# Attention of an adaLN block: row blocks in the outer loop in place of head groups, with the output projection at two-unit spacing and the modulation sums among the projections

## The chip, the cores and the metric

The kernel runs on one core of a Trainium2 chip. The metric is the device time of one execution in microseconds. Engines are called as the profile names them: PE (TensorE, matrix products), DVE (VectorE), ACT (ScalarE), POOL (GpSimd) and SP (SyncE, which issues most of the transfers).

## The reference

The input x has 2048 rows of 576 numbers. Six modulation vectors come from one conditioning row. Attention has 32 heads of 18 numbers and a causal window of 256 rows; then comes a spatial-shift mixer and an MLP (hidden width 4608).

```python
mod = (silu(c) @ w_mod).reshape(1, 6, 1, -1)
sa, ca, ga, sb, cb, gb = (mod[:, n] for n in range(6))
h = layernorm(x) * (1 + ca) + sa
q, k, v = split(h @ wqkv)                # 32 heads of 18
p = softmax(where(0 <= i - j < 256, q @ k.T * 18 ** -0.5, -1e9))
x = x + ga * ((p @ v) @ wo)              # output projection
h = layernorm(x) * (1 + cb) + sb
x = x + gb * B(h)                        # shift mixer, then gelu MLP
```

## The kernel before

The 2048 rows are 16 row tiles of 128 and, for attention, four row blocks g = 0 to 3 of 512. The 32 heads are four groups c = 0 to 3 of eight; each group has two halves hq of four heads. All fp32 products are made of three split (high and low) products.

**Projections.** Normalised rows are multiplied with the V, Q and K weights (`vproj` L406, `qproj` L422). Q and K go to DRAM (`qkh`, `qkl`).

**Attention.** One unit is one (c, g, hq), 32 in all. `uload` (L451) brings its Q and K with 12 transfers on SP's queue into a tile U, of which there are four. `s2` makes 16 score products `sc` (PE, L477) and their row maxima (DVE, L484); then the maxima go into the U tile (`mr` on DVE, L490 and L491). `s3` of the unit makes the products `X` (L526, L527), the exponentials (ACT, L533), `av` (PE, L548) and the copy `avs` (ACT, L553), and transposes and normalises the result into the tile `o`. `s3` of one unit runs beside `s2` of the next. With the second half of a head group, `o` is stored to DRAM as `od`[g] (L570). A block g=0 has only 512 rows of keys, the others 768. Before the change the loops are c outside, g inside, hq innermost, so unit n is 8c + 2g + hq: units 0, 1, 8, 9, 16, 17, 24 and 25 have g=0, and the output rows of every block are complete only in the last head group.

**Output projection.** `s4(g, i)` does row tile t = 4g + i in steps at the offsets `d4`, in units of about 12 us: load `or` from `od` and the input row tile `xr` (SP); transposes `oTT` (PE L68 and L72, with ACT copies and DVE L70, L74); two halves of 14 matmuls with `Wo` (PE L763) and the additions to `xr` (DVE L764); store `xp`; row statistics; modulation in two DVE instructions (L99, then L101, `ln1`); store `hbd`; statistics; normalisation (L886, `ln2`); store `xnd`. The three stores are L769 on SP. `woload` multiplies the rows of `Wo` with `ga` and splits them (POOL). The steps of block 3 are played in the next stage.

**Modulation.** `modvec(v)`, v = 2 to 5, loads five chunks of `w_mod`, multiplies and adds them on POOL, sums over partitions with four matmul records on PE (L215) and stores the vector.

**What sets the order.** Each step is an event with a time in units; `play()` emits them in the order of these times. For PE, POOL and SP the written order is the program order. For DVE and ACT the framework's scheduler chooses it. A transfer on SP whose data isn't ready holds all transfers written behind it.

Of the kernel before, what the change touches and what calls it, by code (L numbers as in the profile page):

```python
# [27 lines left out]
NCH = H // CH  # L28
# [22 lines left out]
class Kern:  # L51
# [54 lines left out]
    def row(self, name):  # L106
        return self.rp.tile([P, D], F32, tag="r", name=name, bufs=self.b_row)
# [19 lines left out]
    def phase_a(self):  # L127
# [9 lines left out]
        NGA = 4  # L137
        self.nb = {"sc": self.b_sc, "st": self.b_st, "tr": 1, "av": 1}
        with ExitStack() as st:
# [11 lines left out]
            units = []  # L151
# [74 lines left out]
            def warm(k):  # L226
                def f():
                    pw = self.ps.tile([P, 512], F32, tag="sc", name=f"pw{k}", bufs=self.b_sc)
                    for _ in range(self.n_warm[k]):
                        nc.tensor.matmul(pw, self.zb, self.zb.unsqueeze(1).to_broadcast([P, 4, P]), start=True, stop=True)  # L230
                return f
# [207 lines left out]
                return f  # L439

            def unit(c, g, hq):
                return units[(2 * g + hq) % 4]

            def uload(c, g, hq):
                def f():
                    q, k = unit(c, g, hq)
                    h0 = 8 * c + 4 * hq

                    def put(dst, row, src, first, r, c0, c1, eng=nc.sync):
                        v = src[first:first + 4 * DH, c0:c1].rearrange("(j r d) n -> d j r n", r=2, d=DH)[:, :, r, :]  # L450
                        eng.dma_start(dst[row:row + DH].bitcast(F32), v)  # L451

                    c0, c1 = max(0, g * 512 - 256), g * 512 + 512
                    kd = k[:, :, 768 - (c1 - c0):]
                    for r in range(2):
                        for n, src in enumerate((qkl, qkh, qkh)):
                            put(kd, 64 * r + n * DH, src, D + h0 * DH, r, c0, c1)
                        for n, src in enumerate((qkh, qkh, qkl)):
                            put(q[:, r::2, :], 64 * r + n * DH, src, h0 * DH, r, g * 512, c1, nc.scalar if c == g == hq == 0 else nc.sync)
                return f  # L460

            KR = P - 2

            def s2(c, g, hq):
                QZ, KZ = unit(c, g, hq)
                box = []
                reds = {}
# [36 lines left out]

            def s3(c, g, hq):
                QZ, KZ = unit(c, g, hq)
                Pb, Xb, abox = {}, {}, []
                banks = [0, 3, 1, 2] if g else [3, 1, 2]
# [114 lines left out]
            s4 = self.s4  # L623

            def sub2(c, g, hq, tb):
                st, f1, f2 = s2(c, g, hq)
                return [(tb + 0.95 * t / 16, f) for t, f in st] + [(tb + 0.96 + 0.06 * self.lt, f1), (tb + 1.05 + self.l_m, f2)]

            def sub3(c, g, hq, tb):
                st, n, f1, f2, f3 = s3(c, g, hq)  # L630
                e = max(t for t, _ in st) / n * self.ww
                return [(tb + self.ww * t / n, f) for t, f in st] + [(tb + e + self.l_f, f1), (tb + e + self.l_f + self.l_o, f2), (tb + e + self.l_f + self.l_o + self.l_s, f3)]
# [3 lines left out]
            T0 = -16.2  # L636
            ev = [(T0 - 1.99, lambda: lns[0][0]()), (T0 - 1.98, consts), (T0 - 1.975, cond), (T0 - 1.97, warm(0))]
# [24 lines left out]
            for kind, a, b in jobs:  # L662
                g = a // 4 if kind == "v" else b
# [14 lines left out]
            for t in range(4, NT):  # L678
                g, i = divmod(t, 4)
                ld, stt, nm, tr = lns[t]  # L680
# [15 lines left out]
                ev.append((ta[n], ualloc(n)))  # L696
            shift = self.t_end + self.u0

            u = 0
            for c in range(NCH):  # L700
                for g in range(NGA):
                    for hq in range(2):
                        tb = 2 * u + hq + shift
                        n = 2 * u + hq
                        tu = tb - self.u_ld
                        ev.append((max(tu, ta[n] + 0.01) if n < 4 else tu, uload(c, g, hq)))
                        ev.append((tb - 0.001, lambda c=c, g=g, hq=hq, tb=tb: sub2(c, g, hq, tb)))
                        ev.append((tb + self.o3 - 0.001, lambda c=c, g=g, hq=hq, tb=tb + self.o3: sub3(c, g, hq, tb)))
                    if c == NCH - 1:
                        for i in range(4 if g < 3 else 0):  # L710
                            t4 = 2 * u + shift + 1.2 + self.o3 + self.ww + self.l_av / 16 + self.l_f + self.l_o + self.l_r + 0.5 * i - self.d4[0]
                            ev += [(t4 + d, f) for d, f in s4(g, i)]
                    u += 1
            uw = 2 * (3 * NGA) - 0.6 + shift
            wb, steps = woload()
            ev.append((uw, wb))
            for k, (ld, ml, sp) in enumerate(steps):
                ev += [(uw + 0.05 + 0.4 * k, ld), (uw + 0.45 + 0.4 * k, ml), (uw + 0.5 + 0.4 * k, sp)]
            for n, v in enumerate((2, 3, 4, 5)):
                steps, spill, store = modvec(v)  # L720
                t0 = shift + 5.0 + 4.2 * n
                for k, (ld, ch) in enumerate(steps):
                    ev += [(t0 + 0.35 * k, ld), (t0 + 0.35 * k + 0.4, ch)]
                ev += [(t0 + 3.7, spill), (t0 + 3.9, store)]
            tw = 2 * u - 0.1 + shift
            wb, steps = self.load_w1()
            ev.append((tw, wb))
            w2 = self.load_w2()
            for n, (ld, f) in enumerate(steps + w2):
                d = 0.17 if n < len(steps) else 0.08  # L730
                t0 = tw + 0.17 * min(n, 10) + 0.08 * max(0, n - 10)
# [4 lines left out]
    def s4(self, g, i):  # L736
        nc, rp, row, Wo = self.nc, self.rp, self.row, self.Wo
        t = 4 * g + i
        box = {}

        def load():
            box["o"] = row(f"or{t}")
            nc.sync.dma_start(box["o"], self.od[g][i * P:(i + 1) * P, :])
            box["x"] = row(f"xr{t}")
            nc.sync.dma_start(box["x"], self.x[t * P:(t + 1) * P, :])

        def tr():
            box["T"] = rp.tile([P, 2 * KC + 1, P], F32R, tag="oT", name=f"oT{t}", bufs=1)
            self.split9(box["o"], box["T"], slice(0, P), f"oTT{t}", ("sc", "st") if g < 3 else ("tr", "tr"))

        def wo(hf):
            def f():
                T, x = box["T"], box["x"]
                cs = slice(hf * 288, (hf + 1) * 288)
                tag = ("sc", "st")[hf] if g < 3 else "mm"
                po = self.ps.tile([P, 288], F32, tag=tag, name=f"po{t}_{hf}", bufs=self.nb[tag])
                pl = []
                for k in range(KC):
                    h, l = Wo["m"][:, k, cs], Wo["m"][:, KC + k, cs]
                    pl += [(T[:, k, :], h), (T[:, k, :], l), (T[:, KC + k, :], h)]  # L760
                pl += [(T[:, 2 * KC, :], Wo["h"][:, cs]), (T[:, 2 * KC, :], Wo["l"][:, cs])]
                for n, (l, r) in enumerate(pl):
                    nc.tensor.matmul(po, l, r, start=(n == 0), stop=(n == len(pl) - 1))  # L763
                nc.vector.tensor_tensor(out=x[:, cs], in0=po, in1=x[:, cs], op=ALU.add)  # L764
            return f

        def put(d):
            def f():
                nc.sync.dma_start(d[t], box["x"])  # L769
            return f  # L770

        def stat(k):
            def f():
                box["s"] = self.stats(box["x"], f"{k}{t}")
            return f

        def ln1():
            x = box["x"]
            self.modulate(x, x, *box["s"], self.cb, self.sb, self.m_s4)

        def ln2():
            x = box["x"]
            self.norm_t(x, x, *box["s"])
        d = self.d4
        return list(zip(d, (load, tr, wo(0), wo(1)))) + [(d[3] + self.l_p, put(self.xp)), (d[4], stat("b")), (d[4] + self.l_n, ln1), (d[4] + self.l_n + self.l_p, put(self.hbd)), (d[5], stat("c")), (d[5] + self.l_n, ln2), (d[5] + self.l_n + self.l_p, put(self.xnd))]
# [395 lines left out]
    u0, u_ld = -1.55, 1.3  # L1181
    e_ld, e_tr, e_w2, e_x1, e_lt, e_s4 = 1.2, 0.7, 1.2, 0.8, 0.8, 0.0
    d4 = (-0.2, 0.1, 0.38, 0.56, 0.85, 1.2)
    l_r = 0.4
    c_w, c_t = 8.1, 8.6
    lt, l_e, l_av, l_f, l_o = 1.2, 0.1, 0.0, 0.1, 0.12
    l_m = 0.1
# [34 lines left out]
```

## Time and profile before

| | |
|---|---|
| median of 3 runs | 1789.46 us (1785.65 to 1795.23) |
| the profiled execution | 1788.75 us, its span 1786.9 us |
| projections, dense on PE | about 20 to 222 us |
| attention units | about 196 to 658 us |
| shift mixer | 688 to 865 us |
| MLP, PE-bound | from 865 us on |

PE is busy for 97% of the span. A stretch in which PE stands or runs at a lower granted clock is thus a stretch of the result. The row `avs` (L553) comes once in each unit and marks the units in time.

### The profile page before, as it was taken

The numbers are of one execution on the slowest core, as the hardware profiler recorded it, in microseconds if no ns is written. First come the engines' busy times: TensorE is split into PE (matmuls) and PEld (weight loads), VectorE is DVE, ScalarE is ACT, GpSimd is POOL, SyncE is SP. The second block draws the span as 40 slices with busy tenths as digits, with TensorE's granted clock in tenths as the row PEclk, the third lists the DMA queues.
The fourth block names the chain that finished last, engine by engine and source line by source line (L and its number), as shares of the span: only waits on it lengthen the run. The fifth ranks groups of instructions, "written<-read, shape, count | busy, mean of one in ns | idle before, by whom it ended". The sixth has DMA issues, their size and how long they took to land.

```text
span 1786.9 us, 30143 instructions
## 1 busy us (share of the span) xinstructions
PE 1731.2 (97%) x11700; PEld 1501.8 (84%) x11700; DVE 977.6 (55%) x2674; ACT 594.5 (33%) x1262; POOL 390.1 (22%) x379
## 2 busy tenths in 40 slices
PE   7999999999998988999899999999999999999999
PEld 5898767677767768899799999999999999999998
DVE  5402387778777875877544444444444444444434
ACT  4622166666664444354211111111111111111111
POOL 5511102222030110201432333234421121122100
PEclk8999999999999997999999999999999999999999
DMA  6434544544444556632211111111110000000002
GB/s 178 122 101 155 181 124 134 136 118 140 119 139 126 172 176 190 202 101 78 86 48 35 42 55 40 36 49 55 55 35 16 29 26 16 29 29 29 1 1 106
DMA packets 97712, 156.88 MB, mean 88 GB/s; under 512 B 11035, under 2 KB 40479, under 8 KB 97571
## 3 DMA queue, kind: packets, MB, share of 16 engines
q1 hardware_dynamic: 86612, 135.12, 25.5%
q10 hardware_dynamic: 10958, 19.85, 3.1%
q8 instruction: 92, 1.51, 0.4%
q14 instruction: 50, 0.40, 0.1%
HBM read 107.06 MB, written 47.20 MB: 86 GB/s over the span
## 4 chain that ended last, share of the span: by engine, by line
PE 55%; DVE 2%; POOL 0%; issue 0%; DMA 0%; ACT 0%; SPq 0%; POOLq 0%; ACTq 0%; DVEq 0%
PE p L1147 26%; PE p L1118 22%; PE p L1120 2%; PE p L1119 2%; PE w L1012 2%; PE pg L959 2%; DVE x L1013 0%; DMA r<-in_B_w_dram 0%; DVE G L977 0%; POOL CW L1102 0%; DVE LNT L70 0%; DVE CW L1097 0%; DVE xm L886 0%; DVE G L964 0%; DVE Gc L1129 0%
## 5 line engine op out<-in xcount | busy, mean ns | idle before, releaser
L1147 PEld LDWEIGHTS p<-CW,Gc 128*128 128x128 f32 x3456 | 473.8, 188 | 16.2 <-DVE Gc L1129 3.7
L1147 PE MATMUL p<-CW,Gc 128*128 128x288 f32 x3456 | 482.0, 295 | 3.5 <-DVE Gc L1129 3.5
L1118 PE MATMUL p<-LNT,CW 128*128 128x512 f32 x1728 | 419.1, 391 | 0.0
L1118 PEld LDWEIGHTS p<-LNT,CW 128*128 128x128 f32 x1728 | 316.2, 188 | 58.8
L1126 ACT ACTIVATE gfc<-p 128x512 f32<-128x512 f32 x144 | 86.2, 599 | 735.5 <-PE p L1120 735.5
L1151 DVE TENSOR_TENSOR acc<-p,acc 128x288 f32<-128x288 f32 x340 | 153.8, 455 | 319.2 <-PE p L1147 315.9
L484 DVE CUSTOM_DVE_ANT_0 sc<-sc,mask 128x384 f32<-128x384 f32 (+2 forms) x512 | 261.8, 555 | 84.1 <-PE sc L477 81.3
L533 ACT ACTIVATE P<-X 128x384 f32<-128x384 f32 x480 | 221.8, 490 | 107.9 <-PE X L527 94.5
L477 PE MATMUL sc<-U 126*128 126x384 f32 (+2 forms) x512 | 197.8, 404 | 5.5 <-DVE m L484 3.9
L526 PE MATMUL X<-U 128*128 128x384 f32 (+2 forms) x704 | 181.9, 317 | 4.8 <-DMA U<-ms 1.9
L1151 DVE TENSOR_TENSOR accw<-p,accw 128x288 f32<-128x288 f32 x204 | 90.0, 453 | 129.5 <-PE p L1147 128.1
L526 PEld LDWEIGHTS X<-U 128*128 128x128 f32 x704 | 126.7, 191 | 35.3 <-issue 23.9
L527 PE MATMUL X<-maskb,identb 128*128 128x256 bf16 x480 | 136.1, 284 | 0.0
L1129 DVE TENSOR_TENSOR Gc<-gfc,Gc 128x512 fp32r<-128x512 f32 x144 | 124.8, 867 | 4.5
L422 PE MATMUL pq<-hT,Wq 128*128 128x512 f32 x504 | 122.0, 400 | 2.3 <-POOL Wq L380 1.6
L422 PEld LDWEIGHTS pq<-hT,Wq 128*128 128x128 f32 x504 | 95.0, 190 | 24.8 <-POOL Wq L380 1.9
L477 PEld LDWEIGHTS sc<-U 126*128 126x128 f32 x512 | 98.5, 197 | 13.4 <-DVE m L484 9.6
L1098 POOL TENSOR_TENSOR CW<-r,CW 128x1024 fp32r<-128x1024 f32 x17 | 41.5, 2440 | 283.2 <-DVE CW L1096 283.2
L548 PE MATMUL av<-P,V 128*32 128x256 f32 (+2 forms) x1472 | 91.0, 379 | 0.0
L1128 ACT CAST Gc<-gfc 128x512 fp32r<-128x512 f32 x144 | 89.4, 621 | 4.6
L1102 POOL TENSOR_TENSOR CW<-r,CW 128x1152 fp32r<-128x1152 f32 x17 | 46.4, 2728 | 158.3 <-DVE CW L1101 158.3
L527 PEld LDWEIGHTS <-identb 128*128 128x128 bf16 x480 | 46.0, 96 | 36.0 <-issue 18.6
(1056 smaller groups left out, 1973.5 us busy)
## 6 DMA issues: line engine op xcount, KB each, us to landing
U<-qkh SPq DMA_DIRECT2D x156, 72.0 KB
U<-qkh SPq DMA_DIRECT2D x96, 108.0 KB
r<-in_B_w_dram SPq DMA_DIRECT2D x18, 576.0 KB
qkh<-hl ACTq DMA_DIRECT2D x36, 256.0 KB
qkl<-hl ACTq DMA_DIRECT2D x36, 256.0 KB
r<-in_B_w_dram SPq DMA_DIRECT2D x18, 512.0 KB
U<-qkl SPq DMA_DIRECT2D x78, 72.0 KB
U<-qkl SPq DMA_DIRECT2D x48, 108.0 KB
```

What stands on the lines that cost most here:

```text
L422: nc.tensor.matmul(pq, a, b, start=(n == 0), stop=(n == len(pl) - 1))
L477: nc.tensor.matmul(sc[:, lo:], QZ[:KR, q, i * P:(i + 1) * P], KZ[:KR, j, i * P + lo:(i + 3) * P], start=True, stop=True)
L484: nc.vector.tensor_tensor_reduce(out=sc[:, lo:], in0=sc[:, lo:], in1=mask[:, lo:], scale=1.0, scalar=-3e38, op0=ALU.add, op1=ALU.max, accu ...
L526: nc.tensor.matmul(X[:, x0:x0 + nb, :].rearrange("p a b -> p (a b)"), KZ[:, j, kb * P:(kb + 1) * P], QZ[:, q, qb * P:(qb + nb) * P], start ...
L527: nc.tensor.matmul(X[:, 0::2, :], self.identb, mk, start=False, stop=True)
L533: nc.scalar.activation(Pb[b][:, q, :], Xb[b, q].rearrange("p a b -> p (a b)"), AF.Exp, scale=SCALE)
L548: nc.tensor.matmul(abox[0][32 * q:32 * q + 32, q0:q0 + w], V[4 * g + kb][:, hv:hv + 32], Pb[b][:, q, p0:p0 + w], start=(first and n == 0), ...
L1118: nc.tensor.matmul(pg, W3[:, ws, fs], L[:, xs, :], start=(i == 0), stop=False)
L1128: nc.scalar.copy(Gh, gf)
L1129: nc.vector.tensor_tensor(out=Gl, in0=gf, in1=Gh.bitcast(F32), op=ALU.subtract)
L1147: nc.tensor.matmul(po, a, w, start=(i == 0), stop=(i == len(seq) - 1))
L1151: nc.vector.tensor_tensor(out=acc[t][:, cs], in0=po, in1=acc[t][:, cs], op=ALU.add)
```

## The change

The loops of attention go over g outside and c inside, so unit n is 8g + 2c + hq, and the first eight units have g=0. The output of block g is complete after its eight units; the four steps s4(g, 0 to 3) for g < 3 are put into the eight units after that, two units apart (before: half a unit apart, all in the last head group). `woload` goes from about unit 23 to unit 2, with steps 0.8 apart in place of 0.4. The four `modvec` sums go from attention into the projections (`t_mv`, `d_mv`). `l_r` goes from 0.4 to 0.5. From about line 700 on, line numbers are smaller by two in the changed kernel: L743 becomes L741, L763 L761, L764 L762, L769 L767.

```diff
             def unit(c, g, hq):
-                return units[(2 * g + hq) % 4]
+                return units[(2 * c + hq) % 4]
...
-            u = 0
-            for c in range(NCH):
-                for g in range(NGA):
+            n = 0
+            for g in range(NGA):
+                for c in range(NCH):
                     for hq in range(2):
-                        tb = 2 * u + hq + shift
-                        n = 2 * u + hq
+                        tb = n + shift
                         tu = tb - self.u_ld
                         ev.append((max(tu, ta[n] + 0.01) if n < 4 else tu, uload(c, g, hq)))
                         ev.append((tb - 0.001, lambda c=c, g=g, hq=hq, tb=tb: sub2(c, g, hq, tb)))
                         ev.append((tb + self.o3 - 0.001, lambda c=c, g=g, hq=hq, tb=tb + self.o3: sub3(c, g, hq, tb)))
-                    if c == NCH - 1:
-                        for i in range(4 if g < 3 else 0):
-                            t4 = 2 * u + shift + 1.2 + self.o3 + self.ww + self.l_av / 16 + self.l_f + self.l_o + self.l_r + 0.5 * i - self.d4[0]
-                            ev += [(t4 + d, f) for d, f in s4(g, i)]
-                    u += 1
-            uw = 2 * (3 * NGA) - 0.6 + shift
+                        n += 1
+                for i in range(4 if g < 3 else 0):
+                    t4 = n - 1 + shift + self.o3 + self.ww + self.l_f + self.l_o + self.l_s + self.l_r + 2.0 * i - self.d4[0]
+                    ev += [(t4 + d, f) for d, f in s4(g, i)]
+            uw = shift + 2.0
             wb, steps = woload()
             ev.append((uw, wb))
             for k, (ld, ml, sp) in enumerate(steps):
-                ev += [(uw + 0.05 + 0.4 * k, ld), (uw + 0.45 + 0.4 * k, ml), (uw + 0.5 + 0.4 * k, sp)]
-            for n, v in enumerate((2, 3, 4, 5)):
+                ev += [(uw + 0.05 + 0.8 * k, ld), (uw + 0.85 + 0.8 * k, ml), (uw + 0.9 + 0.8 * k, sp)]
+            for v in (2, 3, 4, 5):
                 steps, spill, store = modvec(v)
-                t0 = shift + 5.0 + 4.2 * n
+                t0 = T0 + self.t_mv + self.d_mv * (v - 2)
                 for k, (ld, ch) in enumerate(steps):
-                    ev += [(t0 + 0.35 * k, ld), (t0 + 0.35 * k + 0.4, ch)]
-                ev += [(t0 + 3.7, spill), (t0 + 3.9, store)]
-            tw = 2 * u - 0.1 + shift
+                    ev += [(t0 + 0.3 * k, ld), (t0 + 0.3 * k + 0.5, ch)]
+                ev += [(t0 + 2.0, spill), (t0 + 2.1, store)]
+            tw = n - 0.1 + shift
...
-    l_r = 0.4
+    l_r = 0.5
+    t_mv, d_mv = 3.6, 2.3
```

In the rows below the number behind a name is the tile (or0, xr0 belong to row tile 0; sc and mr carry c, g, hq, then bank and quarter), and the last number is the buffer's own. First SP's queue before the change, from the load of row tile 1 to that of row tile 3:

```order
L743 DMA or1_7147<-od0_130 128x576
L745 DMA xr1_7149<-in_A_x_dram 128x576
L769 DMA xp0_114<-xr0_7038 128x576
L743 DMA or2_7285<-od0_130 128x576
L745 DMA xr2_7287<-in_A_x_dram 128x576
L769 DMA hbd0_82<-xr0_7038 128x576
L769 DMA xp1_115<-xr1_7149 128x576
L451 DMA U3_2171<-qkl_139 18x2x768
```

Behind these come the other eleven loads of U3 (unit 31), the store `xnd0` and the load `or3`. SP's queue after the change, from the store of `hbd0` to the load of row tile 1, while unit 12 (c=2, g=1, hq=0) is under way on PE; U1 is the tile of unit 13:

```order
L767 DMA hbd0_82<-xr0_3726 128x576
L451 DMA U1_2049<-qkl_139 18x2x768
L451 DMA U1_2049<-qkh_138 18x2x768 x2
L451 DMA U1_2049<-qkh_138 18x2x512 x2
L451 DMA U1_2049<-qkl_139 18x2x512
L451 DMA U1_2049<-qkl_139 18x2x768
L451 DMA U1_2049<-qkh_138 18x2x768 x2
L451 DMA U1_2049<-qkh_138 18x2x512 x2
L451 DMA U1_2049<-qkl_139 18x2x512
L767 DMA xnd0_98<-xr0_3726 128x576
L570 DMA od1_131<-o0_1_3818 128x4x144
L741 DMA or1_4162<-od0_130 128x576
```

The loads of row tiles 1 and 2, which stood ahead of the first stores of row tile 0, now come behind all of them and behind a whole U load. VectorE before the change, around the modulation of row tile 0 (unit 29 in its scores):

```order
L87 BN_AGGR b0mv_7293<-b0st_7292 128x2
L70 TENSOR_TENSOR oT1_7238<-oTT1pa_7239,oT1_7238 128x512
L74 TENSOR_TENSOR oT1_7238<-oTT1pb_7246,oT1_7238 64x128
L99 SCALAR_TENSOR_TENSOR xr0_7038<-xr0_7038,b0mv_7293,cb_6143 128x576
L484 ISA sc3_2_1_0_3_7263,m3_2_1_7188<-sc3_2_1_0_3_7263,mask_165 128x384
L484 ISA m3_2_1_7188 128x1
```

And after the change, from the last maximum of unit 11 to the second of unit 12:

```order
L484 ISA sc1_1_1_3_3_4081,m1_1_1_3872<-sc1_1_1_3_3_4081,mask_165 128x384
L484 ISA m1_1_1_3872 128x1
L490 TENSOR_SCALAR mr1_1_1_4098<-m1_1_1_3872 128x4x4
L99 SCALAR_TENSOR_TENSOR xr0_3726<-xr0_3726,b0mv_3961,cb_2347 128x576
L491 SCALAR_TENSOR_TENSOR mr1_1_1_4098<-m1_1_1_3872,mr1_1_1_4098 128x4x4
L484 ISA sc2_1_0_0_0_4095,m2_1_0_4094<-sc2_1_0_0_0_4095,mask_165 128x384
L484 ISA m2_1_0_4094 128x1
L101 SCALAR_TENSOR_TENSOR xr0_3726<-xr0_3726,b0rs_3962,sb_2346 128x576
L484 ISA sc2_1_0_0_1_4101,m2_1_0_4094<-sc2_1_0_0_1_4101,mask_165 128x384
```

L99 and L101 of row tile 0, which stood in the middle of a unit's maxima beside the transposes of row tile 1, now stand around the end of unit 11 and the first score of unit 12. PE before the change, the transposes of row tile 1:

```order
L763 MATMUL po0_1_7219<-Wom_6140,oT0_7084 128x288 x12
L763 MATMUL po0_1_7219<-Woh_6141,oT0_7084 128x288
L763 MATMUL po0_1_7219<-Wol_6146,oT0_7084 128x288
L477 MATMUL sc3_2_1_0_2_7236<-U1_1945 128x384
L68 MATMUL oTT1pa_7239<-ident_71,or1_7147 128x128 x4
```

And after the change:

```order
L477 MATMUL sc2_1_0_2_1_4197<-U0_1963 128x384
L526 MATMUL X1_1_1_0_1_4200<-U3_2275 128x128
L526 MATMUL X1_1_1_0_1_4200<-U3_2275 128x256
L527 LDWEIGHTS identb_78
L527 MATMUL X1_1_1_0_1_4200<-maskb_166,identb_78 128x2x128
L477 MATMUL sc2_1_0_2_2_4205<-U0_1963 128x384
L68 MATMUL oTT1pa_4211<-ident_71,or1_4162 128x128 x4
```

The transposes of row tile 1 stood right behind the matmuls of row tile 0; now they stand behind the 11th of the 16 scores of unit 12, nearly two units behind the transposes of row tile 0.

## Prediction

> **What bounds the kernel now.** I read the page's first lines, then one row that comes once in each attention unit, then a table of stretches, and last the queue of SP around the output projection.
>
> ```profile
> span 1786.9 us, 30143 instructions
> PE 1731.2 (97%) x11700; PEld 1501.8 (84%) x11700; DVE 977.6 (55%) x2674; ACT 594.5 (33%) x1262; POOL 390.1 (22%) x379
> ```
>
> TensorE is busy for 97%, so a microsecond in which it waits is a microsecond of the result, and no other engine is near. The sum below is made against the profiled execution, 1788.75 us (span 1786.9 and 1.85 around it); the median of the runs, 1789.46, is 0.7 above it.
>
> ScalarE copies the `av` sums to `avs` (L553) once per unit, so the starts of these copies are a clock of the units. Before the change, units 8 and 9 (g=0) end at the first two rows, 19 and 23 at the next two, 24 and 31 at the last two:
>
> ```profile
> 329.44 0.59 ACT L553 COPY avs<-av 128x512 f32<-128x512 f32 x1 [1.25 <-PE av L548]
> 340.71 0.59 ACT L553 COPY avs<-av 128x512 f32<-128x512 f32 x1 [1.25 <-PE av L548]
> ...
> 461.86 0.59 ACT L553 COPY avs<-av 128x512 f32<-128x512 f32 x1 [1.22 <-PE av L548]
> 509.67 0.59 ACT L553 COPY avs<-av 128x512 f32<-128x512 f32 x1 [1.22 <-PE av L548]
> 522.13 0.59 ACT L553 COPY avs<-av 128x512 f32<-128x512 f32 x1 [1.26 <-PE av L548]
> ...
> 658.18 0.59 ACT L553 COPY avs<-av 128x512 f32<-128x512 f32 x1 [0.91 <-PE av L548]
> ```
>
> A full unit takes (509.67−461.86)/4 = 11.95 us. The seven units up to 658.18 take 136.05, or 19.4 each, because the projection steps s4 stand among them. Where that time goes, the stretches show (columns: stretch, its length, busy time and count by engine, granted clock of TensorE, DMA share, GB/s):
>
> ```profile
> core 0: us, PE busy (x) PEld busy (x) DVE busy (x) ACT busy (x) POOL busy (x), PEclk, DMA share, GB/s
> 414.60:509.70 95.10, 93.22 (x860) 67.70 (x859) 75.48 (x290) 62.72 (x137) 20.14 (x19) 1.00 0.49 139
> 522.10:658.20 136.10, 124.96 (x1052) 99.40 (x1053) 106.40 (x345) 66.50 (x160) 14.21 (x34) 0.99 0.51 155
> 658.20:687.70 29.50, 19.19 (x101) 16.32 (x100) 18.87 (x51) 7.80 (x21) 4.93 (x12) 0.75 0.63 191
> 546.50:549.90 3.40, 0.04 (x1) 0.00 (x0) 0.71 (x4) 0.40 (x1) 0.00 (x0) 0.99 0.50 157
> 549.90:553.30 3.40, 3.34 (x15) 3.07 (x16) 1.55 (x5) 1.58 (x4) 0.00 (x0) 0.51 0.60 160
> 666.30:671.90 5.60, 0.04 (x2) 0.03 (x1) 3.19 (x10) 0.43 (x1) 1.56 (x4) 0.77 0.88 260
> 671.90:679.60 7.70, 7.24 (x29) 6.56 (x30) 2.74 (x8) 2.09 (x6) 0.00 (x0) 0.50 0.79 244
> 869.00:872.50 3.50, 0.09 (x1) 0.00 (x0) 1.78 (x3) 0.68 (x2) 1.59 (x3) 1.00 0.65 176
> 872.50:876.00 3.50, 3.46 (x24) 3.14 (x25) 2.82 (x7) 0.84 (x2) 2.15 (x1) 1.00 0.29 90
> ```
>
> Quiet attention (first row) leaves TensorE idle for 1.88 us in eight units. In the projection zone it idles for 11.1 us, and in the 29.5 us between the last attention unit and the dense part of the next stage for 10.3, with 0.75 of the clock in what it does run. The last six rows are three gaps, each with the stretch behind it: after 3.4 us of waiting the clock stood at 0.51 for 3.4 us, after 5.6 us at 0.50 for 7.7 us, and after 3.5 us at 869 it did not fall.
>
> **What the change gives back.** One s4 has 28 matmuls on TensorE besides its transposes:
>
> ```profile
> 649.45 1.84 PE L763 MATMUL po<-Wom,oT 128*128 128x288 f32 x12
> L763 PE MATMUL po<-Wom,oT 128*128 128x288 f32 x229 | 35.4, 302 | 1.2 <-DVE m L484 0.8 <-DVE b3mv L87 0.4
> ```
>
> Twelve in 1.84 us, the last of 0.30, are 0.14 us from start to start, so 28 take 3.9; with about 0.3 for transposes I put an s4 at 4.2 us. The 267 matmuls of the zone (229 of this kind and 19 each of the two others) are 9.55 steps. 136.05 − 7×11.95 − 9.55×4.2 = 12.3 us are lost there. Of the 29.5 us behind it, the idle 10.3 and a quarter of the busy 19.19 (4.8) are 15.1 lost; I let 5 stay, since the next stage must still fetch its first operands, and count 10. Spread steps could give back these 22 us. Bounds: 0 (waits go elsewhere) and 27.
>
> Grouping all eight g=0 units at the front: the one from 329.44 to 340.71 takes 11.27, and the one before it 10.5; a pair beside full ones saves about 2.1 us, four pairs 8.5. Eight in a row at 10.5 save 11.6. Gain 3, bounds 0 and 5.
>
> The four `modvec` sums move from attention into the projections, with their matmuls:
>
> ```profile
> 307.97 1.14 PE L215 MATMUL pm<-wm,ones 128*128 128x288 f32 x4
> ```
>
> Four times 1.14 us leave one TensorE-bound stretch and enter another. Five `w_mod` loads and one store for each of the four sums leave SP's queue between U loads and enter it between the weight loads of the projections, which are read one piece ahead. Loads and POOL steps stand ahead of the matmuls by half a unit or more, so I take 0; bounds −1 and +3, where a sum reached TensorE before its POOL steps. `woload` moves from unit 23 to the units from 2 on: five row loads and three broadcasts enter SP's queue between U loads, and the POOL work is covered by an engine busy for 22%. I take 0; without that cover one U load would be late by 8 issues of about 0.4 us, 3 us in all, once.
>
> **What the change costs.** TensorE and SP both run their instructions strictly in the written order. In the changed kernel, SP has between two s4 steps: store `hbd`(i), the 12 loads of the next U, store `xnd`(i), store `od`, and only then `or`(i+1). TensorE has the transposes of `or`(i+1) right behind the 11th of 16 scores of the same unit. VectorE reaches L101, which `hbd`(i) needs, only behind all 16 maxima of the unit before and the first of this one. How long each link takes, these rows show; first the start of a unit (22) on TensorE and VectorE, then L99 and L101 from the zone:
>
> ```profile
> 466.30 0.63 PE L477 MATMUL sc<-U 126*128 126x384 f32 x2
> 466.92 0.17 DVE L490 TENSOR_SCALAR mr<-m 128x16 fp32r<-128x16 f32 x1
> 467.13 0.17 DVE L491 SCALAR_TENSOR_TENSOR mr<-m,mr 128x16 fp32r<-128x16 f32 x1
> 467.22 0.56 DVE L484 CUSTOM_DVE_ANT_0 sc<-sc,mask 128x384 f32<-128x384 f32 x1
> ...
> 578.85 0.82 DVE L99 SCALAR_TENSOR_TENSOR xr<-xr,b1mv,cb 128x576 f32<-128x576 f32 x1
> 580.07 0.81 DVE L101 SCALAR_TENSOR_TENSOR xr<-xr,b1rs,sb 128x576 f32<-128x576 f32 x1
> ```
>
> With S the start of unit 12's scores: `mr` at S+0.6, L99 from 0.8 to 1.6, the second `mr` to 1.8, the first maximum to 2.3, L101 to 3.1. Then the queue. The same sequence stands once in the kernel before (SP rows: issue time, issue duration):
>
> ```profile
> 544.52 0.39 SPq L570 DMA_DIRECT2D od<-o  x1
> 547.16 0.35 SPq L743 DMA_DIRECT2D or<-od  x1
> ...
> 574.96 0.30 SPq L451 DMA_DIRECT2D U<-qkl  x1
> ...
> 581.11 0.27 SPq L451 DMA_DIRECT2D U<-qkl  x1
> 581.42 0.34 SPq L769 DMA_DIRECT2D xnd<-xr  x1
> 581.97 0.34 SPq L743 DMA_DIRECT2D or<-od  x1
> ```
>
> Twelve U loads hold SP from 574.96 to 581.38, 6.4 us, and `or` is issued 0.6 us behind them. And what the reader then waits:
>
> ```profile
> L68 PE MATMUL oTT0pa<-ident,or x4: 421/421/447, 550.0 to 550.6; 128*128 128x128 f32 x4
> L68 PE MATMUL oTT3pa<-ident,or x4: 272/273/300, 587.2 to 587.6; 128*128 128x128 f32 x4
> PE oTT3pa L68 <- DMA or<-od: 1.7, 1, 1.7
> ```
>
> `or` issued at 547.16 on an empty queue is read at 550.0 (2.8 us), `or` issued at 581.97 behind U loads at 587.2 (5.2 us), in both with TensorE waiting for it. So in the changed kernel `hbd` goes at S+3.1, U from 3.5 to 9.9, `xnd` 9.95, `od` 10.5, `or` 10.95, and it lands between S+13.75 and S+16.15. TensorE wants it at 11/16 of 11.95, S+8.2. The wait is 5.5 to 7.9 us; with L101 and the loads each about a microsecond sooner it would be 3.8. I take 6.5, between the two landings, as the queue is like that of 581.97 but has one 288 KB load fewer. Eight steps (i = 1 to 3 of each block, without the last, behind which no U is left to load) pay it: 52 us. The first steps of blocks 1 and 2 read an `od` that is stored directly ahead of them; from 544.52 to 547.16 `or` waited 2.6 us for that, so 9.1 each, 18. The very first finds no `hbd` ahead of it, only the wait for its `od`, which is stored directly ahead too; I take 5, less than the others. Together 75 us, bounds 48 (3.8 and 6.4 each) and 89 (7.9 and 10.5).
>
> All eleven gaps are over 3.4 us, and then the clock comes in. By the rows above a gap costs 1.7 us (half of 3.4), 3.85 (half of 7.7) or nothing. I take 1.7, the middle row: 19 us; bounds 0 and 42.
>
> The Trainium skill, page "TensorE: Matmul & The Clock Gate", section "What's actually happening", has the array fall to half clock after an idle window of about 3.4 us and come back after about as long a busy one; by it each of these gaps would lose half of one window, some 19 us in all (an estimate). The rows at 546 agree with it; the 5.6 us gap, which cost 7.7 us at half clock, and the 3.5 us gap, which cost nothing, don't.
>
> While TensorE stands, ScalarE and VectorE get ahead, which saves its own small waits: 0.24 us per unit in the quiet row, two units per step, 5 us in all. Other VectorE work of s4 lies beside attention, at 71% in the quiet stretch; without that cover it would lengthen the same wait.
>
> Sum: +75 + 19 − 5 − 22 − 3 = +64, so 1788.75 + 64 = about 1852 us. Lowest 48 − 5 − 27 − 5 + 0 = +11 (1800), highest 89 + 42 − 5 − 22 − 3 = +101 (1890).
>
> **The rivals.**
> 1. Faster: `or` lands before S+8.2. This needs SP to reach it 6 us sooner: L101 is done before unit 12 starts, or the U loads were issued in the unit before. Nothing holds VectorE but the order of its instructions, and its load is 71%, which speaks for it; the place of L101 speaks against it. Then the gains alone count: 1788.75 − 25 = 1764.
> 2. No change within 0.5%, which is about what a measurement of this kernel can tell from no change. The gains of 30 (22, 3 and 5) are eaten by 2.7 us per step. That is less than half of the wait that I derive, and can come if `or` lands 2.8 us after issue and U loads take 4 us instead of 6.4: about 1789. Waits longer than this make it slower.
> 3. Half clock as behind the 5.6 us gap, at each step: 75 + 42 in place of 75 + 19, 1875. For it speaks that all waits are near 5.6 or longer; against it that scores and X matmuls follow densely, where at 671.9 a short s4 stood alone.
> 4. The steps don't get spread at all, as the waits push them together again: 1789 and no gain. The order on TensorE excludes it.
>
> **How the numbers follow.** Slower by the waits as summed, 1852: 0.66, its own range 1800 to 1875. Rival 3, 1875: 0.15. Faster, 1764: 0.13; the links are few and each is read from a row, but I hold orders of three engines together by hand. No change: 0.06. So faster 0.13, same 0.06, slower 0.81. The range leaves out rival 1 and the outer end of rival 3: 1790 to 1885.
>
> **What the profile after would show.** In the chain and in the waits: eleven rows of `oTT` transposes waiting for DMA `or<-od`, 5 to 9 us each, about 75 in all. In the copies to `avs`: units alternating between 12 and about 24 us from the 10th on, and under 11 for the first eight. On SP: each `or` 0.6 to 1.1 us behind the last of twelve U loads. Clock: below 1.00 behind each gap. In the projections: no wait of L215 on POOL. If `or` is issued before the U loads end, or the transposes don't wait, the sum falls with its largest term, and the kernel is faster by up to 25 us.

## The result, and the profile after

The changed kernel takes 1877.93 us (median of 4 runs, 1876.79 to 1878.46), the kernel before 1791.17: a ratio of 1.0488, 95% interval 1.0474 to 1.0502. It is slower by 87 us; forecast were 1852 us and a range from 1790 to 1885. The profiled execution has a span of 1875.0 us, 88.1 more than before.

First the page of the changed kernel, to hold against the three rows of before:

```profile
span 1875.0 us, 30124 instructions
PE 1750.6 (93%) x11700; PEld 1516.1 (81%) x11700; DVE 976.9 (52%) x2674; ACT 597.4 (32%) x1262; POOL 387.6 (21%) x379
```

The count of matmuls is the same, 11700. PE is busy for 19.4 us more (1750.6 against 1731.2) and idle for 68.7 us more (124.4 against 55.7). These two numbers are the whole loss, and the rest of this section puts them in place. The waits of PE, by what ended them (total, times, longest):

```profile
PE oTT8pa L68 <- DMA or<-od: 8.2, 1, 8.2
PE oTT4pa L68 <- DMA or<-od: 7.8, 1, 7.8
PE oTT9pa L68 <- DMA or<-od: 6.9, 1, 6.9
...
PE oTT2pa L68 <- DMA or<-od: 5.8, 1, 5.8
PE oTT3pa L68 <- DMA or<-od: 5.8, 1, 5.8
...
PE oTT0pa L68 <- DMA or<-od: 3.4, 1, 3.4
```

There are eleven such rows, 65.4 us in all. Before the change three of them made 10.7 us. What holds the load, the waits of SP's queue over the whole program show, first before, then after the change:

```profile
SPq L769 <- DVE xr L764: 37.3, 10, 7.0
SPq L769 <- DVE xr L101: 24.6, 10, 4.5
```

```profile
SPq L767 <- DVE xr L101: 122.6, 14, 11.4
SPq L767 <- DVE xr L762: 98.5, 13, 12.2
```

The same stores, `hbd` and `xp`, made SP stand for 62 us before and for 221 us now. (Before the change, the load of row tile 2 stood ahead of `hbd0` but behind `xp0`, as the order of the queue shows, and not ahead of both.) One step from the timeline, around unit 16 (s4 of row tile 2 behind it, row tile 3 ahead); PE, VectorE, SP and PE again:

```profile
426.21 0.62 PE L477 MATMUL sc<-U 126*128 126x384 f32 x2
```

```profile
426.90 0.81 DVE L99 SCALAR_TENSOR_TENSOR xr<-xr,b2mv,cb 128x576 f32<-128x576 f32 x1
...
428.19 0.81 DVE L101 SCALAR_TENSOR_TENSOR xr<-xr,b2rs,sb 128x576 f32<-128x576 f32 x1
```

```profile
429.04 0.34 SPq L767 DMA_DIRECT2D hbd<-xr  x1
429.47 0.30 SPq L451 DMA_DIRECT2D U<-qkl  x1
...
435.53 0.32 SPq L451 DMA_DIRECT2D U<-qkl  x1
435.94 0.34 SPq L767 DMA_DIRECT2D xnd<-xr  x1
436.33 0.43 SPq L570 DMA_DIRECT2D od<-o  x1
436.81 0.56 SPq L741 DMA_DIRECT2D or<-od  x1
```

```profile
430.80 0.44 PE L477 MATMUL sc<-U 126*128 126x384 f32 x1 [0.29 <-DVE c2mv L87]
...
432.96 0.45 PE L477 MATMUL sc<-U 126*128 126x384 f32 x1 [0.34 <-DVE m L484]
...
435.68 0.42 PE L477 MATMUL sc<-U 126*128 126x384 f32 x1
441.88 0.66 PE L68 MATMUL oTT3pa<-ident,or 128*128 128x128 f32 x2 [5.79 <-DMA or<-od]
```

From the unit's first score at 426.2, L101 ends 2.8 us later, `hbd` is issued at +2.8, the U loads hold SP from +3.3 to +9.6, `or` is issued at +10.6, and PE, which was ready at +9.9, starts at +15.7.

Last the stretches: the first eight units of attention and the rest of attention with all s4 steps up to the dense part of the mixer, of before and of after; then, of after, what lies between the last unit and the dense part, and the 6 us behind one wait.

```profile
195.60:298.70 103.10, 98.48 (x766) 72.25 (x765) 76.21 (x289) 53.34 (x115) 15.95 (x14) 0.98 0.50 146
298.70:684.90 386.20, 360.42 (x3153) 272.19 (x3152) 298.04 (x1068) 217.96 (x492) 63.49 (x84) 0.98 0.49 143
```

```profile
200.10:293.90 93.80, 85.22 (x694) 62.67 (x692) 66.96 (x289) 44.90 (x97) 23.80 (x19) 1.00 0.51 157
293.90:774.50 480.60, 390.05 (x3210) 293.25 (x3209) 305.20 (x1069) 228.31 (x508) 18.94 (x48) 0.90 0.37 106
761.60:774.50 12.90, 3.49 (x14) 2.14 (x14) 7.31 (x24) 5.24 (x15) 0.79 (x2) 0.62 0.57 169
403.60:409.60 6.00, 6.00 (x28) 5.70 (x29) 3.59 (x11) 2.64 (x6) 0.00 (x0) 0.50 0.59 146
```

The first eight units are 9.3 us shorter, the second stretch is 94.4 us longer. In it, PE idles for 90.6 us in place of 25.8, and is busy for 29.6 us more. About 13.3 of these are work that left the first stretch (its eight units have smaller blocks now), and the four `modvec` sums, 4.6 us, have gone from it. The rest is the half clock: 0.90 is granted over the whole stretch. Taken together, the stretches at 0.50 behind the eleven waits are these; the shortest, the longest, and the sum of all eleven:

```profile
676.10:679.40 3.30, 3.30 (x15) 2.99 (x16) 1.53 (x5) 1.56 (x4) 0.00 (x0) 0.50 0.60 141
403.60:409.80 6.20, 6.20 (x29) 5.90 (x29) 3.79 (x11) 2.71 (x6) 0.00 (x0) 0.50 0.59 145
sum 50.20, PE 50.13 PEld 46.87 DVE 28.40 ACT 21.51 POOL 0.00; mean PE 4.56 PEld 4.26 DVE 2.58 ACT 1.96 POOL 0.00
```

PE works for 50.1 us at half clock behind these waits, 4.6 us each. At the full clock it would take about half of that, so some 25 us are lost there (an estimate from these rows).

### The profile page after: what moved, and what is told of

It is laid out like the page before. It is cut to its first block, busy times and chain, and to the rows that moved or that the text cites. A ratio compares the mean times of both kernels' runs of the same rounds, so it can differ in the third digit from the quotient of the medians.

```text
span 1875.0 us, 30124 instructions
## 1 busy us (share of the span) xinstructions
PE 1750.6 (93%) x11700; PEld 1516.1 (81%) x11700; DVE 976.9 (52%) x2674; ACT 597.4 (32%) x1262; POOL 387.6 (21%) x379
## 4 chain that ended last, share of the span: by engine, by line
PE 77%; DMA 10%; DVE 8%; POOL 2%; ACT 2%; issue 2%; SPq 1%; ACTq 0%; DVEq 0%; POOLq 0%
PE p L1145 24%; PE p L1116 21%; PE pq L422 5%; PE X L526 4%; PE sc L477 3%; PE av L548 3%; PE po L761 3%; DMA or<-od 2%; DVE sc L484 2%; DMA U<-ms 2%; PE X L527 2%; PE pg L957 2%; PE pv L406 2%; PE w L1010 2%; PE p L1118 2%; PE p L1117 2%
## 5 line engine op out<-in xcount | busy, mean ns | idle before, releaser
L477 PE MATMUL sc<-U 126*128 126x384 f32 (+2 forms) x512 | 202.3, 417 | 10.7 <-DVE m L484 6.8
L526 PE MATMUL X<-U 128*128 128x384 f32 (+2 forms) x704 | 188.0, 327 | 9.7 <-DMA U<-ms 6.0
L526 PEld LDWEIGHTS X<-U 128*128 128x128 f32 x704 | 135.0, 205 | 39.2 <-issue 23.0
L527 PE MATMUL X<-maskb,identb 128*128 128x256 bf16 x480 | 140.7, 293 | 0.0
L477 PEld LDWEIGHTS sc<-U 126*128 126x128 f32 x512 | 101.8, 205 | 19.4 <-DVE m L484 14.8
L527 PEld LDWEIGHTS <-identb 128*128 128x128 bf16 x480 | 47.6, 99 | 38.3 <-issue 21.8
```

The lines of the kernel that those rows point to most:

```text
L477: nc.tensor.matmul(sc[:, lo:], QZ[:KR, q, i * P:(i + 1) * P], KZ[:KR, j, i * P + lo:(i + 3) * P], start=True, stop=True)
L526: nc.tensor.matmul(X[:, x0:x0 + nb, :].rearrange("p a b -> p (a b)"), KZ[:, j, kb * P:(kb + 1) * P], QZ[:, q, qb * P:(qb + nb) * P], start ...
L527: nc.tensor.matmul(X[:, 0::2, :], self.identb, mk, start=False, stop=True)
```

## Experiments

Ratios are against the kernel before, with 95% intervals. The changed kernel is at 1.0488.

**Take eight of the eleven waits away.** Only the loads of `or` and `xr` are moved ahead in SP's queue; everything else stays.

```diff
-                    ev += [(t4 + d, f) for d, f in s4(g, i)]
+                    ev += [(t4 + d - (1.0 if k == 0 and i else 0.0), f) for k, (d, f) in enumerate(s4(g, i))]
```

> The changed kernel with one edit: for i = 1 to 3 the loads of or and xr stand one unit earlier in SP's queue, ahead of the store hbd(i-1) and of the 12 U loads. Theory (queue): the eight waits of 5.0 to 6.9 us (45.9 in all) go, and the half clock behind them (some 3 us each, 24); the three first steps keep 3.4, 7.8 and 8.2. 1878 - 70 = about 1808 us. Rival (next in line): U loads still stand behind hbd and land at about S+14, so the first scores of the next unit wait in their place, 3 to 5 us per step: 1840 to 1860. Rival (VectorE): PE then waits for L70/L74 or the additions, since VectorE is late as well: 1850 or more.

1819.55 us, 1.0156 (1.0139 to 1.0172). No transposes of i = 1 to 3 wait any more; this alone brings back 58 us, about the 45.9 of waits and their half clock, or two thirds of the loss. It was 12 us above the 1808 expected. The first steps still wait, and there is a new entry:

```profile
PE sc L477 <- DVE m L484: 15.3, 23, 2.7
PE oTT4pa L68 <- DMA or<-od: 9.2, 1, 9.2
PE oTT8pa L68 <- DMA or<-od: 9.1, 1, 9.1
```

Scores that wait for VectorE's maxima rose from 6.8 us in the changed kernel to 15.3. The queue theory holds, and neither of the rivals reached its size.

**Move the steps, not the loads.**

```diff
-    l_r = 0.5
+    l_r = 0.85
```

> The changed kernel with l_r 0.85 in place of 0.5: all steps of s4 0.35 unit later against attention. In SP's order the U loads then stand ahead of hbd, and or(i+1) follows hbd, od and xnd directly; on PE the transposes stand at the end of the unit, not behind its 11th score. Theory (queue): or is issued at about S+7 and lands by S+12, when PE wants it, so eight waits go; the first steps keep 0 to 4 us each. 1878 - 58 - 27 = about 1793 us. Rival (any wait of hbd on VectorE holds the next or, wherever it stands): waits of 3 us or more stay, 1830 or more.

1851.46 us, 1.0339 (1.0324 to 1.0355): a miss of 58 us. The U loads do stand ahead of `hbd` now, yet ten waits of 4.7 to 6.6 us stay. SP's rows say why:

```profile
429.67 0.34 SPq L767 DMA_DIRECT2D hbd<-xr  x1
430.06 0.43 SPq L570 DMA_DIRECT2D od<-o  x1
437.25 0.33 SPq L767 DMA_DIRECT2D xnd<-xr  x1
437.62 0.43 SPq L741 DMA_DIRECT2D or<-od  x1
```

```profile
436.65 0.57 DVE L884 TENSOR_SCALAR xr<-xr,c2mv,c2rs 128x576 f32<-128x576 f32 x1
```

SP stood from 430.5 to 437.25 for `xnd`, which needs L884, and VectorE's order had put L884 late. The next load behind any store of the step waits for VectorE, not only the one behind `hbd`. This was the rival.

**Take the half clock away.** Twenty products of bf16 identities, whose result is overwritten, fill PE while it would wait:

```diff
+        if tags[0] == "sc":
+            for _ in range(20):
+                nc.tensor.matmul(pa, self.identb, self.identb.unsqueeze(1).to_broadcast([P, KC, P]), start=True, stop=True)
```

> The changed kernel with 20 products of bf16 identities (128x128 by 128x512, results overwritten) on PE ahead of the transposes of each s4 in attention, some 4 to 5 us in which PE would stand. The loads and their waits end when they did. Theory (clock): PE never idles for long, the granted clock stays at 1.00, and the stretches of 5.4 to 6.1 us at half clock behind ten or eleven waits become half as long: 1878 - 30 = about 1848 us, with or waits of 1 to 4 us left. Rival (the half clock doesn't come from the gap but from the work behind it, or waits cost the same either way): 1876 to 1885.

1872.9 us, 1.0463 (1.0442 to 1.0484); 1848 was expected. In the stretch from one s4 to the next (row tiles 2 and 3) the clock did what the theory says:

```profile
406.40:444.80 38.40, 33.87 (x277) 23.85 (x277) 24.12 (x85) 17.41 (x38) 1.58 (x4) 1.00 0.38 109
```

The clock stands at 1.00, but the stretch is 38.4 us long, where the changed kernel took 38.3 with 0.90. At the end of this one, 20 products of 4.5 us and 3.1 us of waiting stand where it waited 5.8. The links of this step can be read off. From the transposes of row tile 2 to the first score of unit 16 it took 20.9 us (406.37 to 427.31), in the changed kernel 22.6 (403.57 to 426.21): the clock gave 1.7. From that score to the next transposes it took 17.5 us in place of 15.7, and 1.8 were taken back: 0.9 by the store `od`, which held SP for 1.37 us in place of 0.43, 0.5 by the landing (5.6 us in place of 5.1) and 0.3 by the U loads. Whether that follows from the full clock isn't shown.

The other steps were not all at full clock. Behind five of the ten waits that are left in this run, of 1.9 to 3.9 us, the clock still stood at 0.50, for 21.5 us of PE work in all, where it was 50.1 in the changed kernel; the mean over the program rose only from 0.970 to 0.983. By these rows the products gave back about 14 us of clock (an estimate, half of the difference), and 5 of them reached the result. So the 30 that were expected were counted too high, and part of what the clock did give went into longer waits.

**The loop order with the old spacing.**

```diff
-+ self.l_r + 2.0 * i - self.d4[0]
++ self.l_r + 0.5 * i - self.d4[0]
```

> The changed kernel with the steps of s4 half a unit apart in place of two units, as before the change; loops, woload and modvec as changed. Then most loads of or stand ahead of hbd as they did before. Theory (queue): few waits, as before the change, but three times the wait of the first step (3.4, 7.8, 8.2) and some late third one (1.7 each time): about 25 us of waits in place of 65, with half clock behind three to six of them: 1878 - 40 - 15 = 1815 to 1830 us. Rival (the loop order itself costs, with U, q/k and od traffic in another order): 1860 or more.

1809.44 us, 1.0104 (1.0089 to 1.0119). This is below the 1815 to 1830 expected. With g outside, `woload` and `modvec` as changed, and only the spacing of before, 68 of the 87 us are gone; six waits for `or` make 16.8 us. The spacing of two units is the costly part of the change. The loops with the rest (`woload`, `l_r` and the place of the first step) cost 19 us here; these were not run apart from each other.

**No wait for `or` at all.** The first experiment's edit, and the first step of each block 0.75 unit later behind its load.

```diff
+                    ev += [(t4 + d + (0.75 if k and i == 0 else -1.0 if i and k == 0 else 0.0), f) for k, (d, f) in enumerate(s4(g, i))]
```

> The changed kernel with or(i) for i = 1 to 3 one unit earlier, and in addition all steps but the load of the first s4 of each block 0.75 unit later, so that its od and or have landed. Theory (queue): no wait of or is left; the three of 3.5, 9.2 and 9.1 us and the half clock behind them (some 8) go too: 1820 - 28 = about 1792 us, no faster than before the change, since some 2.3 us per step stay that aren't loads (scores that wait for VectorE's maxima, for L99 and L101 stand among them). Rival (the first waits are paid elsewhere, in the steps that move closer to their successors): 1810 or more. Rival (spreading gives back what the prediction counted, 25 us): 1770.

1807.54 us, 1.0084 (1.0066 to 1.0103). No row of `oTT` in attention waits for a load. Yet the kernel is 16 us slower than before the change, where I expected no difference; that is nearer to the first rival (1810) than to the theory:

```profile
PE sc L477 <- DVE m L484: 12.8, 18, 2.0
PE X L526 <- DMA U<-ms: 11.3, 10, 2.1
PE xnT1pa L1055 <- DVE T L912: 6.3, 1, 6.3
PE sc L477 <- DMA U<-qkl: 6.0, 6, 2.2
...
PE xnT0pa L1055 <- DVE o L566: 2.7, 1, 2.7
...
PE sc L477 <- DMA U<-qkh: 1.8, 2, 1.6
```

```profile
294.80:708.30 413.50, 373.90 (x3211) 276.50 (x3210) 305.71 (x1069) 225.55 (x508) 19.01 (x48) 0.97 0.42 124
```

In the same stretch PE now idles for 39.6 us, against 25.8 before the change. Moving `or` ahead in SP's queue left the U loads behind `hbd`, and they and the small transfer `ms` became late. The kernel before has 3.9 us in the first of these rows, 1.9 in that of `ms`, none for the U loads, and 2.0 at the first two tiles of the mixer (`xnT0`, `xnT1`), where 9.0 stand now: some 33 us of other waits came, and the 10.7 for `or` went. In this placement the spread does not give back 25 us.

**Packed steps with early loads.** The spacing of 0.5, loads 0.3 unit earlier, other steps 0.75 later.

```diff
-+ 2.0 * i - self.d4[0]
-                    ev += [(t4 + d, f) for d, f in s4(g, i)]
++ 0.5 * i - self.d4[0]
+                    ev += [(t4 + d + (0.75 if k else 0.0 if i == 0 else 0.45), f) for k, (d, f) in enumerate(s4(g, i))]
```

> The changed loops with the steps of s4 half a unit apart, as in e5, the loads of i = 1 to 3 0.3 unit earlier, and all other steps 0.75 unit later. Theory: the or waits of e5 (3.7, 3.6, 3.6, 2.1, 2.0, 1.8) go, with half clock behind some of them: 1809 - 17 - 3 = about 1789 us. If packed steps lose by themselves (PE waits for L70, L74 and the additions), 1795 or more; if loops and modvec bring what they promise, below 1785.

1807.61 us, 1.0079 (1.0059 to 1.0099), as good as the one before it and 19 us above the theory. The third row tile of each block still waits (2.3 to 2.5 us), U loads are late by 5.3 us. Two different ways to place twelve steps end at the same 16 us.

**`modvec` alone**, put into the kernel before.

```diff
-                t0 = shift + 5.0 + 4.2 * n
+                t0 = T0 + self.t_mv + self.d_mv * (v - 2)
...
```

> The kernel before with only the modvec part of the change (the four sums among the projections), loops, s4 and woload as before. Theory of the prediction: same work in another PE-bound stretch, 0 with bounds -1 and +3, so 1789 to 1794 us. Rival: the loads in the projections make PE wait there, +5 or more.

1790.0 us, 0.9990 (0.9978 to 1.0001): no difference, as priced.

**The stores on another queue.** The written order stays, and POOL issues `xp`, `hbd` and `xnd`.

```diff
-                nc.sync.dma_start(d[t], box["x"])
+                (nc.gpsimd if g < 3 else nc.sync).dma_start(d[t], box["x"])
```

> The changed kernel with one edit: the three stores of s4 in attention (xp, hbd, xnd) are issued by POOL and no longer by SP. Every load keeps its place in SP's order, and VectorE's order is as it was. Theory (SP stands at hbd until VectorE has done L101, and U and or queue behind it): or 1 to 3 are now issued before unit S begins, their eight waits go, U loads and ms aren't late either (the 7.8 and 11.3 us seen where only the or loads were moved); the first or of each block keeps 3.4, 7.8, 8.2. 1876 - 46 - 24 - 10 = about 1796 us. Rival (the loads are slow by their traffic, 12 U loads and 5 us of landing, whoever issues the stores): waits of 3 us and more stay, 1840 or more.

1899.31 us, 1.0612 (1.0597 to 1.0627): slower than the change by 21 us, where I expected a gain of 80. The waits for `or` are smaller (2.4 to 4.0 us), and another wait has taken their place:

```profile
PE sc L477 <- DVE m L484: 40.3, 27, 3.9
```

```profile
DVE xr L884 <- DMA hbd<-xr: 39.9, 13, 4.0
```

L884 writes `xr` in place, so it must wait until the store `hbd` has read it. In the changed kernel the same row of waits was 1.7 us in all. One step of each, first of the changed kernel, where `hbd` was issued at 429.04 (above):

```profile
431.80 0.58 DVE L884 TENSOR_SCALAR xr<-xr,c2mv,c2rs 128x576 f32<-128x576 f32 x1
```

```profile
429.49 0.64 POOL L767 DMA_DIRECT2D hbd<-xr  x1 [1.73 <-DVE xr L101]
434.79 0.58 DVE L884 TENSOR_SCALAR xr<-xr,c2mv,c2rs 128x576 f32<-128x576 f32 x1 [3.50 <-DMA hbd<-xr]
```

From SP the store had read `xr` at most 2.8 us behind its issue, since L884 didn't wait. From POOL it took 5.3 us. In SP's queue the store went ahead of the U loads; here SP issues them around it. For these loads as the reason speaks that `xp` and `xnd`, which POOL issues too, landed 2.4 and 2.5 us behind their issue (medians of the twelve) and only `hbd` took 5.2; it was not tried by itself. Two things changed, not one: VectorE's order, which the scheduler chooses, is another as well, although I expected it to stay. L99, L101 and L884 now stand in the middle of a unit's maxima, some ten maxima sooner, and L884 comes two maxima behind L101 where it was four. So VectorE stands with scores behind it. How much of the 39.9 us is the later landing and how much the new place isn't separated.

And SP isn't free either:

```profile
SPq L451 <- DMA U<-ms: 169.1, 18, 15.8
SPq L451 <- PE X L527: 67.0, 7, 12.0
```

By the profile's semaphore events, one of the U loads waits for the transfer `ms`, which ScalarE issues; in the changed kernel this row says 53.0 us, and in the kernel before 107.4. So in this run the U loads, and `or` behind them, did not run ahead of the unit although no store held SP.

**Both: stores on POOL, first steps later.**

```diff
+                (nc.gpsimd if g < 3 else nc.sync).dma_start(d[t], box["x"])
...
+                    ev += [(t4 + d + (0.75 if k and i == 0 else 0.0), f) for k, (d, f) in enumerate(s4(g, i))]
```

> As with the stores on POOL, and in addition all steps but the load of the first s4 of each block 0.75 unit later. Theory: no or wait left, no U or ms wait: the 19 us of the three first steps and the half clock behind two go as well, 1796 - 26 = about 1770 us, below the kernel before: the spread itself would then give what the prediction counted. Rival (scores that wait for VectorE's maxima behind L99 and L101, about 1 to 2 us per step, and the start of the mixer remain): 1785 to 1795, no gain from the spread.

1873.46 us, 1.0461 (1.0448 to 1.0475). The level is as wrong as that of the run before. The step between the two, 25.9 us, meets the 26 that were expected from the first steps, but by luck: in the run before, the three first steps waited for 11.6 us and not for 19.4; all waits for `or` together fell from 34.8 us to 15.3, since those of the second steps went as well.

**The same stores in the kernel before**, with the diff of the stores alone.

> The kernel before with the same edit (stores xp, hbd, xnd of the steps in attention on POOL). Theory: its or waits of 1.7 and 5.6 us shrink, the first (3.4, waiting for od) stays: 1791 - 5 to 10 = 1781 to 1787 us. Rival (in the packed steps the stores don't hold SP): 1789 to 1793.

1805.49 us, 1.0082 (1.0065 to 1.0098). Neither theory: slower by 15 us. VectorE waits for `hbd` for 5.3 us and for `xp` for 8.9 (1.4 and 1.6 with SP), and scores wait for L70 for 9.5 us, a row that the kernel before doesn't have.

**The kernel before with earlier loads.**

```diff
+                            ev += [(t4 + d - (0.25 if k == 0 and i else 0.0), f) for k, (d, f) in enumerate(s4(g, i))]
```

> The kernel before with one edit: the loads of or and xr for i = 1 to 3 a quarter unit earlier. Its own waits for or are 3.4 (i=0), 1.7 (or3) and 5.6 us (or11). Theory (queue): the last two go, with half clock behind the last (3.9): 1790 - 11 = about 1780 us. Rival (the loads were late for another reason, at the end of attention the stage's weight loads fill the queue): or11 keeps 3 us or more, 1786 to 1790.

1787.85 us, 0.9979 (0.9966 to 0.9992): two of its three waits for `or` are gone, but a wait of 4.9 us for VectorE stands at the fifth row tile, and of 11 us expected 4 came.

**And its first step 0.3 unit later.**

```diff
+                            ev += [(t4 + d + (0.3 if k and g == i == 0 else -0.25 if k == 0 and i else 0.0), f) for k, (d, f) in enumerate(s4(g, i))]
```

> The kernel before with the loads of or and xr for i = 1 to 3 a quarter unit earlier and, in addition, all steps but the load of the very first s4 0.3 unit later, so that its od and or have landed. Theory: the first wait (3.5 us) and the half clock behind it (1.7) go: 1788 - 5 = about 1783 us. Rival (steps of the first and second row tile now stand close together and PE waits for L70 and the additions, or VectorE's stores come later): 1787 or more.

1785.94 us, 0.9965 (0.9953 to 0.9978), the fastest of all: 6 us below the kernel before. One wait for `or` of 6.2 us has come to the fifth row tile, so this placement isn't at its end.

## Why the prediction was right, and where its sum was not

The direction, the mechanism and its places were right: eleven waits for `or`, ten of them behind L101, `hbd` and twelve U loads (two of these also behind `od`), and the very first, as forecast, behind `od` alone. The copies to `avs` stand about 10.6 us apart in the first eight units, and from the ninth copy on about 13 us and 22 to 27 us in turn, up to the last three. The sum said 64 us from 1788.75 and the profile shows 88.1. Term by term:

- **The waits**: 75 expected, 65.4 measured. The eight ordinary ones were 5.0 to 6.9 us against 6.5, the first steps 3.4, 7.8 and 8.2 against 5, 9.1 and 9.1. In the step shown above the chain ran as worked out (L101 done at +2.8 against 3.1, U loads 6.4 us, `or` at +10.6 against 10.95). Two sizes in it were off and nearly cancelled. The landing took 5.1 us, the slow end of the two rows and not the middle. And PE wanted the load at +9.9, not +8.2: in unit 22 of the kernel before, the eleventh score starts at +8.3, here at +9.5. Two scores wait for VectorE on the way (430.80 and 432.96 above), which has L101, L85 to L87 and L884 of the same step between the maxima.
- **The clock**: 19 expected, 1.7 for each wait. It was more, about 2.3 for each and 25 in all, as the rows at 0.50 show. PE's busy time grew by 19.4 net, because half clock of before went away: 0.75 was granted in the 29.5 us behind the last unit, and the prediction had that share in the next term. So the agreement of 19 with 19.4 is luck. The run with dummy products shows, too, that the clock can't simply be added to the waits: of about 14 us that it gave, 5 came back.
- **Given back by the spread, 22, with 5 for the engines that get ahead**: these terms failed. Apart from the waits for `or`, PE idled for 45.0 us before (55.7 − 10.7) and 59.0 after (124.4 − 65.4), 14 more. Even if the 10.7 us of old waits, which the 22 contained, are counted as given back, 3 us more of idle time stand there and not some 20 less. The step that failed is the one where the lost time in the old zone was taken as freed by the spacing. Of the stretch behind the last unit I let 5 us stay and counted 10 as gain; PE idled there for 10.3 us before and idles for 9.4 after (761.6 to 774.5), now for the first two tiles of the mixer. In attention other waits came, as the run without any `or` wait shows: on U loads, `ms` and maxima. It stays 16 us behind.
- **Units with g=0 in a row, 3**: the first eight units became 9.3 us shorter, but about 13.3 us of PE work only moved behind them, and PE idled there for 8.6 us in place of 4.6. No gain shows there; whether some of it came elsewhere isn't shown.
- **`modvec`, 0**: the run of it alone agrees.

Reckoned as differences: 54.7 of waits for `or`, 14 of other idle time and 19.4 of busy time, by these rows mostly half clock, are the 88.1.

Two slips in the working bear on this. VectorE's load in the quiet stretch was read as 71%; that is the column of the weight loads (67.70 of 95.10 us), and VectorE's is 75.48, or 79%. So there was less cover for its work of s4 than I took, and its late maxima show in the wait above. And the bounds of the gains reached down to 0, but the highest sum, 1890, still had 25 us of them in it; with 0 it would have been 1915.

On the rivals: that no step waits (1764) wasn't near; even the kernel without these waits doesn't reach 1791. The half clock as a rival (1875) came nearest to the time, but by luck: it had 3.85 us lost at each wait, measured are about 2.3, and what it had too much there, the gains that didn't come made up for.

The Trainium skill, page "TensorE: Matmul & The Clock Gate", section "HAM oscillation — how this bites in real kernels", describes this shape: a wait for a transfer longer than its window puts the array back to half clock at every turn of the loop. The trace agrees on the fall: 0.50 behind each of the eleven waits, from 3.4 to 8.2 us. The return took 3.3 to 6.2 us of work. Filling the wait kept 1.00 in six of eleven places and not in the other five, and it brought back 5 us of 87, so the fall was not what cost most here.

What stays open: why both placements without the large waits end 16 us above the kernel before. The waits that stand there are named, but none was taken away by itself, and neither the loop order nor `woload` was run alone.

## What to carry to other kernels

Where one queue in program order carries both loads that an engine will need and stores that wait for another engine, count for each load the stores ahead of it: here TensorE stood for nearly 6 us, eight times, because a store ahead of the load waited for VectorE. When such a stall is removed, ask what else stood behind the same store; here the U loads became late, and with other waits they kept the kernel 16 us above the one before. Time lost around a bunch of steps isn't a gain of spreading them until the spread order's own waits have been counted.

## What the runs showed of the hardware that was not expected

With the three stores on another issuing engine, the store `hbd` had read its tile 5.3 us behind its issue in the step shown, where it took at most 2.8 us from SP, and the kernel was 21 us slower; VectorE's order changed with it, so the 21 us are not the price of the queue alone. Behind the eleven waits the clock needed 3.3 to 6.2 us of dense work to return from 0.50, without a plain relation to the length of the wait: 3.3 us behind one of 6.9, 6.2 behind one of 5.8. With dummy products in front, waits of 1.9 to 3.9 us were still followed by 0.50 in five places.
